# Four layers of windowed and full attention on one core: moving column maxima, first stores and the second keys

## The chip, the cores and the metric

The kernel runs on one core of a Trainium2 chip. A core has a matrix engine (PE), a vector engine (DVE), an engine for activation functions (ACT), a general engine (POOL) and an engine that here only starts transfers (SP). The engines run side by side, each through its own queue in order, and wait for each other by semaphores. Sixteen DMA engines move data between the core's memory and DRAM. Matrix products land in PSUM, a small memory of banks; a product may only start when the bank it writes has been read out.

The metric is the device time of one execution in microseconds. Before the change the median of three runs is 2730.53 us (2721.45 to 2735.32).

## The reference

The input is one sequence of 2048 rows of 512 numbers. Four layers are applied in turn: windowed (A), full (B), A, B, where the two A layers share their weights and so do the two B layers. A layer normalizes each row, projects to queries, keys and values (32 heads of 16), computes attention, projects with `wo` and adds the result to its input.

```python
def _B_ref(x, wqkv, wo):
    B, S, D = x.shape
    H = 32; Dh = D // H
    qkv = (lambda x, *d: x.transpose(*d))((x @ wqkv).reshape(B, S, 3, H, Dh), 2, 0, 3, 1, 4)
    q, k, v = qkv[0], qkv[1], qkv[2]
    scores = jnp.einsum("bhqd,bhkd->bhqk", q, k) * Dh ** -0.5
    p = _softmax(scores, axis=-1)
    o = jnp.einsum("bhqk,bhkd->bhqd", p, v)
    return (lambda x, *d: x.transpose(*d))(o, 0, 2, 1, 3).reshape(B, S, D) @ wo

x = A_x
x = x + _A_ref(_layernorm(x, axis=-1), A_wqkv, A_wo)
x = x + _B_ref(_layernorm(x, axis=-1), B_wqkv, B_wo)
x = x + _A_ref(_layernorm(x, axis=-1), A_wqkv, A_wo)
x = x + _B_ref(_layernorm(x, axis=-1), B_wqkv, B_wo)
```

`_A_ref` is the same with a mask: a query sees itself and the 255 rows before it.

## The kernel before

**Tiling.** The 2048 rows are cut into four columns (`c` = 0 to 3) of 512 queries. Heads are taken four at a time: `qd` = 0 to 7 counts these groups, and two of them in a row make a head pair's output `oh` (named `O[l, c, t]`, t = qd // 2). A layer's attention runs over c, then qd (in layer 3 over pairs of qd first). In a full layer one (c, qd) has 16 steps, one for each tile of 128 keys; in a windowed layer it has 3. A step computes scores on PE into a PSUM tile `s` (line 667), exponentials `e` on ACT (L671), in windowed layers masks on POOL (L734, L737), and two steps later the product with the values into the bank `acc` (L711 full, L744 windowed). At the end of a qd DVE transposes the sums (`ot`, L639), divides, and after every second qd writes `oh` (L652 to L655).

**Side work.** The projections of the next columns and layers are cut into pieces and laid between the steps by a planner (`Side`), which keeps a clock of estimated microseconds, gives each piece a cost, and takes the next one that is ready by its dependencies. Such a piece is a tile of 12 matmuls (L379 in windowed layers and in the prologue, L376 in full ones). `PH["run"]` says after how many matmuls of it a step of attention may follow: 12 in layer 0, 4 in layer 2. In full layers all side products go through one bank, `acc[1]`: the next tile's first matmul waits until DVE or ACT has copied the tile before out of it. Copies of values are L592 (ACT) and L594 (DVE, `vt`), of queries and keys L487 (ACT) or L489 (DVE) and L490 (DVE, `sp`).

Only PE's order is fixed by the planner. The order of the other engines, SP's transfers among them, is chosen by the framework's scheduler from the order of writing, priorities and its own estimates.

**Prologue.** Before the attention of layer 0, the kernel normalizes column 0, splits three weight matrices of type A into two half-precision parts (`parts`; matrix 1 holds the keys' weights, 0 the queries', 2 the values'), stores them to DRAM for later use (`wd`, L293, on SP's queue), computes keys, queries and values of column 0, and normalizes column 1. All loads and stores go through SP's queue, in order: where one waits, those behind it wait. The keys, queries and values of column 1 (`K(0,1)`, `Q(0,1)`, `VV(0,1)`, 48 matmuls each) are side work of column 0's attention. `kw` and `qs` are the DRAM homes of keys and queries, from which each qd loads `kt` and `qt` (L697 to L700 windowed, L684 to L688 full). `kt` has three buffers and `qt` two; x tiles have four.

**Column maxima.** The kernel checks that every column of the eight weight matrices has its largest magnitude in a range. `column_maxima` loads a matrix of 1 MB (`wq`, L277; the `wo` matrices in eight pieces, L282), after a tiny copy into the buffer (L275) that ties the load to another result; reduces it on DVE in four parts (`wa`, L311), transposes (L315) and reduces again (L317). All eight are work of the first half of layer 1's column 0, as two chains, and their loads are tied to the key maxima `KM[1]`, which are ready when layer 0's tail ends. In that half of layer 1 the upper value heads are side work too: 12 tiles, copied out by L594.

Of the kernel before, what the change touches and what calls it, by code (L numbers as in the profile page):

```python
# [11 lines left out]
F16 = mybir.dt.float16  # L12
# [7 lines left out]
P = 128  # L20
# [12 lines left out]
HEAD_START = 100  # L33
EB, XB, XNB, WB, VB, OB = 6, 4, 4, 2, 3, 5
RUN = 4
# [154 lines left out]
def fast_path(ctx, tc, flag, a_x, a_wqkv, a_wo, b_wqkv, b_wo, out):  # L190
# [29 lines left out]
    def wait(us):  # L220

        return "wait", clock[0] + us
# [62 lines left out]

    def parts(ty, s, raw):

        w = wp.tile([P, NC, 2, D], F16, name=f"w{ty}_{s}", tag="vf", bufs=NQ)
        for k in range(NC):
            nc.scalar.activation(w[:, k, 0, :], raw[:, k, :], AF.Copy, scale=UP[s])  # L290
            nc.vector.scalar_tensor_tensor(w[:, k, 1, :], raw[:, k, :], UP[s], w[:, k, 0, :], op0=ALU.mult, op1=ALU.subtract)
            yield
        nc.sync.dma_start(wd[ty, s], w)  # L293
        if ty == 0 and s < 3:
            WT[ty, s] = [w, w]
# [7 lines left out]
    def column_maxima(ty, s):  # L303

        yield wait(12)
        raw = load_w(ty, s, "vw", "wq", KM[1][:, NQ - 1:])
        yield wait(14)
        am = vp.tile([P, D], F32, name=f"wa{ty}_{s}", tag="am", bufs=1)
        for h in range(4):
            f = slice(h * P, (h + 1) * P)  # L310
            nc.vector.tensor_reduce(am[:, f], raw[:, :, f].rearrange("p k f -> p f k"), axis=AX.X, op=ALU.max,  # L311
                                    apply_absolute_value=True)
# [367 lines left out]
    def load_full(l, c, qd):  # L680
        n = f"{l}_{c}_{qd}"
        pair = slice(2 * qd, 2 * qd + 2)
        qt = pp.tile([P, 2, QC], F16, name=f"qt{n}", tag="qt", bufs=2)
        nc.sync.dma_start(qt, qs[1, c][pair].rearrange("r p n -> p r n"))  # L684
# [7 lines left out]
    def load_win(l, c, qd):  # L692
        n = f"{l}_{c}_{qd}"
        kt = pp.tile([P, 2, S // 2], F16, name=f"kt{n}", tag="kt", bufs=3)
        qt = pp.tile([P, 2, QC], F16, name=f"qt{n}", tag="qt", bufs=2)
        pair = slice(2 * qd, 2 * qd + 2)
# [205 lines left out]
    def run(g):  # L902
        for _ in g:
            pass
# [8 lines left out]
    def attention(l, works):  # L913
# [5 lines left out]
        for t in range(NHT if l == 3 else 1):  # L919
            for c in range(NQ):  # L920
# [9 lines left out]
                if win:  # L930
                    PH["run"] = RUN if l else 12
                ops = load(l, c, qds[0])
# [78 lines left out]
    def PR(ty, s, after=()):  # L1011
        return Work(prep(ty, s), 0.0, ("P", ty, s), after, aside=True)
# [18 lines left out]
    for i in range(4):  # L1031
# [6 lines left out]
        nc.vector.tensor_tensor(xl, pt, xh, ALU.subtract)  # L1038
    run(parts(0, 1, raw[1]))
    xs = load_x(0, 1)  # L1040
    run(keys(0, 0, True, None, True))
    run(parts(0, 0, raw[0]))
    for i in range(4):
# [4 lines left out]
    run(queries(0, 0, True))  # L1048
    run(parts(0, 2, raw[2]))
    vals = values(0, 0, True)  # L1050
# [3 lines left out]
    for d in [("P", 0, i) for i in range(3)] + [("K", 0, 0)]:  # L1054
        DONE[d] = 0.0

    def F(*parts):
# [7 lines left out]
    def side0(c):  # L1065
        if c == 0:
            return [F((kw[1], True), (qs[0, 1], False), (kw[2], True), (qs[0, 2], False)), K(0, 1), Q(0, 1), PR(0, 3, [("K", 0, 1)]), VV(0, 1), PR(1, 1, [("V", 0, 1, (0, 1), 0)]), NN(2, [("T", 0, 1)]), T(0, 2)]
        if c == 1:
# [38 lines left out]
    for i, m in enumerate(mats):  # L1107
        works[1][0].append(CM(*m, [("C", *list(mats)[i - 2])] if i > 1 else []))
    late = lambda l: [("N", l, 3)]
# [55 lines left out]
```

## Time and profile before

| What | Value |
|---|---|
| median of three runs | 2730.53 us (2721.45 to 2735.32) |
| profiled execution | 2732.19 us, of which the span from first to last instruction 2730.5 us |
| PE busy | 2607.2 us (95%), 24315 matmuls |
| ACT busy | 2371.7 us (87%) |
| DVE busy | 853.0 us (31%) |
| POOL busy | 521.9 us (19%) |
| mean granted PE clock | 0.989 |
| DMA | 353.14 MB, mean 129 GB/s |
| scores begin in layer 0, 1, 2 | 52.5 us, 477.8 us, 1449.8 us |

A row of the profile in order of time gives the start in microseconds from the span's start, the length of the merged group, engine and line, the operation, what it writes and reads, how many instructions were merged, and in brackets the idle time of the engine before it with what ended that time. The page's slices cut the span into 40 parts of 68 us; each digit is a busy share in tenths. Matmuls overlap, so a busy PE is not a PE at its peak. A row of the waits gives the waiting engine and line, what ended the wait, the total, the number of times and the longest.

### The profile page before, as it was taken

The page shows a single profiled execution, that of the slowest core. Times are in us where ns is not written, and L with a number is a line of the kernel's source. Part 1 is how long each engine was busy: PE and PEld are TensorE (multiplying, and loading weights), DVE is VectorE, ACT ScalarE, POOL GpSimd, SP SyncE. Part 2 cuts the span into 40 slices and gives each one's busy share as a digit, 9 for nine tenths or more (in the row PEclk, how much of TensorE's full clock was granted, in tenths as well). Part 3 has the DMA queues.
Part 4 walks back from the last instruction along what each step waited for, and adds up shares of the span by engine and source line. Part 5 has one row for each costly group of instructions (what it writes and reads, how often), then busy time and mean ns, then how long its engine had stood idle before and what let it go on. Part 6 is the DMA issues. An engine that isn't in the chain of part 4 may idle for free.

```text
span 2730.5 us, 59472 instructions
## 1 busy us (share of the span) xinstructions
PE 2607.2 (95%) x24315; PEld 758.9 (28%) x24315; DVE 853.0 (31%) x1941; ACT 2371.7 (87%) x2683; POOL 521.9 (19%) x1154
## 2 busy tenths in 40 slices
PE   7889999899999999999999999899999999999998
PEld 3233344222222222222223333422222222222221
DVE  6457454512121112111215576311222221121111
ACT  4566663799999999999997777499999999999997
POOL 1556551000000000000005688100000000000000
PEclk9999999899999999999999999999999999999999
DMA  8777866522232123212324666523333333333331
GB/s 271 226 233 242 243 201 213 159 78 85 86 101 88 58 90 109 79 69 82 109 73 136 195 171 177 159 76 101 110 113 127 126 108 111 95 110 115 99 95 56
DMA packets 322715, 353.14 MB, mean 129 GB/s; under 512 B 114432, under 2 KB 234496, under 8 KB 316416
## 3 DMA queue, kind: packets, MB, share of 16 engines
q1 hardware_dynamic: 322432, 349.25, 42.1%
q8 instruction: 192, 3.15, 0.5%
q14 instruction: 91, 0.75, 0.1%
HBM read 236.45 MB, written 96.99 MB: 122 GB/s over the span
## 4 chain that ended last, share of the span: by engine, by line
PE 74%; ACT 8%; DVE 7%; issue 5%; DMA 4%; SPq 1%; POOL 1%; ACTq 0%; DVEq 0%
PE acc L711 30%; PE s L667 20%; PE acc L376 10%; PE b L379 9%; ACT e L671 7%; PE acc L744 4%; PE bs L379 1%; DVE ot L639 1%; DVE wa L311 1%; DMA wv<-wd 1%; DVE xh L424 1%; DMA kt<-kw 1%; DVE xn L418 1%; DVE sp L490 1%; DMA qt<-qs 0%
## 5 line engine op out<-in xcount | busy, mean ns | idle before, releaser
L671 ACT ACTIVATE e<-s 128x1024 f32<-128x1024 f32 (+2 forms) x2432 | 2246.3, 1120 | 127.3 <-PE s L667 106.3
L711 PE MATMUL acc<-e,vt 128*17 128x512 f32 x8192 | 1082.4, 600 | 5.7 <-DVE ot L639 4.6
L667 PE MATMUL s<-qt,kt 64*128 64x512 f16 (+3 forms) x5504 | 774.6, 356 | 60.6 <-ACT e L671 23.9
L667 PEld LDWEIGHTS <-kt 64*128 64x128 f16 x5504 | 201.6, 94 | 807.3 <-issue 772.2
L737 POOL TENSOR_SCALAR_AFFINE_SELECT e<-e 128x256 f32<-128x256 f32 x512 | 229.5, 455 | 102.4 <-ACT e L671 101.7
L711 PEld LDWEIGHTS acc<-e,vt 128*17 128x17 f32 x8192 | 136.4, 95 | 384.3 <-issue 351.0
L639 DVE STREAM_TRANSPOSE ot<-acc 128x512 f32<-128x512 f32 x128 | 91.6, 715 | 455.2 <-PE acc L711 337.4
L734 POOL TENSOR_SCALAR_AFFINE_SELECT e<-e 128x256 f32<-128x256 f32 x448 | 201.7, 455 | 92.1 <-ACT e L671 88.5
L744 PE MATMUL acc<-e,vt 128*17 128x384 f32 (+2 forms) x2816 | 195.1, 390 | 0.0
L379 PE MATMUL b<-xc,w 128*128 128x512 f16 x700 | 166.2, 385 | 5.1 <-DVE km L528 4.9
L655 POOL TENSOR_TENSOR oh<-o,oh 128x512 f16<-128x512 f32 x31 | 36.0, 1161 | 706.6 <-DVE oh L654 643.3
L596 POOL TENSOR_SCALAR vt<-vt 128x16 f32<-128x16 f32 (+1 forms) x96 | 24.5, 256 | 475.9 <-DVE vt L594 306.5
L376 PE MATMUL acc<-xc,w_h 128*32 128x512 f16 x1296 | 108.5, 379 | 2.3 <-DVE km L528 2.3
L489 DVE TENSOR_SCALAR sp<-acc 128x512 f16<-128x512 f32 x28 | 19.3, 689 | 290.6 <-PE acc L376 278.9
L376 PE MATMUL acc<-xc,w 128*32 128x512 f16 x1344 | 108.9, 379 | 0.0
L487 ACT ACTIVATE sp<-b 128x512 f16<-128x512 f32 x59 | 35.3, 598 | 84.3 <-PE b L379 74.5
L489 DVE TENSOR_SCALAR sp_h<-acc 128x512 f16<-128x512 f32 x27 | 18.6, 690 | 283.5 <-PE acc L376 283.5
L627 DVE SCALAR_TENSOR_TENSOR x<-acc,x 128x512 f32<-128x512 f32 x60 | 41.5, 692 | 206.1 <-PE acc L376 198.2
L379 PEld LDWEIGHTS <-w 128*128 128x128 f16 x800 | 73.6, 99 | 114.5 <-issue 37.3
L376 PE MATMUL acc<-wv,xc 128*32 128x256 f16 (+1 forms) x1728 | 94.8, 313 | 9.8 <-DVE vt L594 9.8
L495 POOL TENSOR_TENSOR sq_h<-sp_h 128x512 bf16<-128x512 f16 x27 | 28.1, 1041 | 389.9 <-DVE sp_h L489 389.9
L376 PE MATMUL acc<-wo,oh 128*32 128x512 f16 x1296 | 101.3, 379 | 0.0
(133 smaller groups left out, 1518.9 us busy)
## 6 DMA issues: line engine op xcount, KB each, us to landing
kt<-kf SPq DMA_DIRECT2D x128, 512.0 KB
qt<-qs SPq DMA_DIRECT2D x128, 256.0 KB
xd<-x SPq DMA_DIRECT2D x96, 256.0 KB
x<-xd SPq DMA_DIRECT2D x96, 256.0 KB
w<-wd SPq DMA_DIRECT2D x20, 1024.0 KB
kt<-kw SPq DMA_DIRECT2D x64, 256.0 KB
qs<-sp SPq DMA_DIRECT2D x48, 256.0 KB
wo<-wd SPq DMA_DIRECT2D x12, 1024.0 KB
```

The source lines that it names most:

```text
L376: nc.tensor.matmul(ps[g:g + 32], a[:, g:g + 32], b, start=(i == 0), stop=(i == len(pairs) - 1), skip_group_check=True)
L379: nc.tensor.matmul(ps, a, b, start=(go and i == 0), stop=(i == len(pairs) - 1))
L489: nc.vector.tensor_scalar(sp[:, 0], ps, e, None, op0=ALU.mult)
L627: nc.vector.scalar_tensor_tensor(xs[i], ps, 1.0 / (UP[2] * UP[3]), xs[i], op0=ALU.mult, op1=ALU.add)
L639: nc.vector.transpose(ot.rearrange("p b r -> p (b r)"), a)
L655: (nc.gpsimd if l % 2 and (l, c, qd) != (3, NQ - 1, NQD - 1) else nc.vector).tensor_tensor(hl[:, 1], o, hl[:, 0], ALU.subtract)
L667: nc.tensor.matmul(ps[:, h, s0:s0 + wd_], kt[R * h:R * h + R, pr, kc:kc + P], qt[R * h:R * h + R, pr, qc:qc + wd_], start=True, stop=True)
L671: nc.scalar.activation(e[:, :, w0:w1], ps[:, :, w0:w1], AF.Exp, scale=SCALE)
L711: nc.tensor.matmul(a[32 * h:32 * h + DH + 1, :], V[l, qd // 4, j // 8][:, j % 8, 4 * (qd % 4) + h, :], es_[h // 2][:, h % 2, :], start=(j ...
L734: nc.gpsimd.affine_select(v, v, pattern=[[0, 2], [-1, P]], compare_op=ALU.is_gt, fill=0.0, base=0, channel_multiplier=1)
L737: nc.gpsimd.affine_select(v, v, pattern=[[0, 2], [1, P]], compare_op=ALU.is_ge, fill=0.0, base=0, channel_multiplier=-1)
L744: nc.tensor.matmul(a[32 * h:32 * h + DH + 1, q * P:(q + nb) * P], V[l, (4 * c + j) // 4][:, j % 4, 4 * qd + h, :], es_[h // 2][:, h % 2, s ...
```

## The change

Five edits:

- `K(0,1)` is run to its end in the prologue, before layer 0's attention, and is no longer side work of column 0.
- The three first stores of split weights are issued on POOL's queue.
- In column 0 of layer 0 side tiles are cut after 4 matmuls, as in layer 2.
- Column maxima i = 0 to 7 are tied to the head pair output `O[1, 0, i // 2]` of layer 1, by planner and by the tiny copy before the load; each odd one also waits for the even one before it. The first two stay in the first half of column 0, the others follow in the rest of the layer.
- `qt` gets three buffers, x tiles five.

```diff
-EB, XB, XNB, WB, VB, OB = 6, 4, 4, 2, 3, 5
+EB, XB, XNB, WB, VB, OB = 6, 5, 4, 2, 3, 5
...
-    def parts(ty, s, raw):
+    def parts(ty, s, raw, eng=None):
...
-        nc.sync.dma_start(wd[ty, s], w)
+        (eng or nc.sync).dma_start(wd[ty, s], w)
...
     def column_maxima(ty, s):
 
-        yield wait(12)
-        raw = load_w(ty, s, "vw", "wq", KM[1][:, NQ - 1:])
+        i = list(mats).index((ty, s))
+        raw = load_w(ty, s, "vw", "wq", O[1, 0, i // 2][:, 0, :1])
...
-        qt = pp.tile([P, 2, QC], F16, name=f"qt{n}", tag="qt", bufs=2)
+        qt = pp.tile([P, 2, QC], F16, name=f"qt{n}", tag="qt", bufs=3)
...
-                    PH["run"] = RUN if l else 12
+                    PH["run"] = RUN if l or not c else 12
...
-    run(parts(0, 1, raw[1]))
+    run(parts(0, 1, raw[1], nc.gpsimd))
...
-    run(parts(0, 0, raw[0]))
+    run(parts(0, 0, raw[0], nc.gpsimd))
...
-    run(parts(0, 2, raw[2]))
+    run(parts(0, 2, raw[2], nc.gpsimd))
...
         DONE[d] = 0.0
+    all_of([K(0, 1)])
...
-            return [F((kw[1], True), (qs[0, 1], False), (kw[2], True), (qs[0, 2], False)), K(0, 1), Q(0, 1), PR(0, 3, [("K", 0, 1)]), VV(0, 1), PR(1, 1, [("V", 0, 1, (0, 1), 0)]), NN(2, [("T", 0, 1)]), T(0, 2)]
+            return [F((kw[1], True), (qs[0, 1], False), (kw[2], True), (qs[0, 2], False)), Q(0, 1), PR(0, 3, [("K", 0, 1)]), VV(0, 1), PR(1, 1, [("V", 0, 1, (0, 1), 0)]), NN(2, [("T", 0, 1)]), T(0, 2)]
...
     for i, m in enumerate(mats):
-        works[1][0].append(CM(*m, [("C", *list(mats)[i - 2])] if i > 1 else []))
+        works[1][0 if i < 2 else 1].append(CM(*m, [("O", 1, 0, i // 2)] + [("C", *list(mats)[j]) for j in (i - 1,) if i % 2]))
```

The edits also move instructions in the queues. The first place is ACT's queue where layer 0's attention begins (`vt` is the last value copy of column 0, `sp_1_1` and `sq_1_1` the copies and squares of the keys of column 1, `e` the exponentials of qd 0). Before:

```order
L592 ACTIVATE vt_0_0_0_461<-b_520 128x32x16
L671 ACTIVATE e_0_0_0_0_546<-s_0_0_0_0_543 128x2x384
L671 ACTIVATE e_0_0_0_1_553<-s_0_0_0_1_550 128x2x384
L487 ACTIVATE sp_1_1_0_580<-b_567 128x512
L671 ACTIVATE e_0_0_1_0_590<-s_0_0_1_0_587 128x2x256
L493 ACTIVATE sq_1_1_0_583<-sp_1_1_0_580 128x512
L671 ACTIVATE e_0_0_1_1_596<-s_0_0_1_1_593 128x2x256
L487 ACTIVATE sp_1_1_1_612<-b_599 128x512
```

After:

```order
L592 ACTIVATE vt_0_0_0_461<-b_520 128x32x16
L487 ACTIVATE sp_1_1_0_548<-bs_535 128x512
L493 ACTIVATE sq_1_1_0_551<-sp_1_1_0_548 128x512
L487 ACTIVATE sp_1_1_1_568<-b_555 128x512
L493 ACTIVATE sq_1_1_1_571<-sp_1_1_1_568 128x512
L487 ACTIVATE sp_1_1_2_588<-bs_575 128x512
L493 ACTIVATE sq_1_1_2_591<-sp_1_1_2_588 128x512
L487 ACTIVATE sp_1_1_3_608<-b_595 128x512
L671 ACTIVATE e_0_0_0_0_626<-s_0_0_0_0_623 128x2x384
L493 ACTIVATE sq_1_1_3_611<-sp_1_1_3_608 128x512
L671 ACTIVATE e_0_0_0_1_633<-s_0_0_0_1_630 128x2x384
```

The copies of the keys stood between the exponentials of qd 0 to 2 and now stand ahead of them, as their matmuls do on PE.

The second place is SP's queue after the fills of the key and query homes, before:

```order
L269 DMA qs_0_97<-ones 32x15x512
L293 DMA wd_1_106<-w_1_206 128x4096
L437 DMA x_4_216<-in_A_x_dram 128x512
L437 DMA x_5_218<-in_A_x_dram 128x512
L437 DMA x_6_220<-in_A_x_dram 128x512
```

and POOL's queue between its constants and the first masks, after:

```order
L253 AFFINE_SELECT hsum<-hsum 128x32
L293 DMA wd_1_106<-w_1_206 128x4096
L293 DMA wd_0_105<-w_0_304 128x4096
L293 DMA wd_2_107<-w_2_451 128x4096
L596 TENSOR_SCALAR vt_0_0_0_461<-vt_0_0_0_461 128x32 x4
L737 AFFINE_SELECT e_0_0_0_0_626<-e_0_0_0_0_626 128x2x128
```

The stores left SP, where x tiles of column 1 stood behind the first of them, for the head of POOL's queue; there the ones beside the values (L596) and the first masks stand behind all three.

The third place is DVE's queue in the first column of layer 1. Before, in qd 0 to 1 (`wq` a loaded matrix, `vt_1_0` copies of values from `acc[1]`):

```order
L594 COPY vt_1_0_5814<-acc_82 128x16x16
L315 STREAM_TRANSPOSE wb_0_7324<-wa_0_7287 128x512
L275 COPY wq_3_7333<-km_3958 128x1
L311 TENSOR_REDUCE wa_1_7289<-wq_1_7175 128x128 x4
L317 TENSOR_REDUCE cmax<-wb_0_7324 128x16
L315 STREAM_TRANSPOSE wb_1_7326<-wa_1_7289 128x512
L317 TENSOR_REDUCE cmax<-wb_1_7326 128x16
L311 TENSOR_REDUCE wa_2_7343<-wq_2_7330 128x128 x4
```

After, behind the output of the first head pair (`oh_0_1`):

```order
L654 CAST oh_0_1_6605<-o_0_1_6603 128x512
L275 CAST wq_0_6678<-oh_0_1_6605 128x1
L275 CAST wq_1_7148<-oh_0_1_6605 128x1
L594 COPY vt_1_0_5814<-acc_82 128x16x16
L311 TENSOR_REDUCE wa_0_6889<-wq_0_6678 128x128 x4
L315 STREAM_TRANSPOSE wb_0_7110<-wa_0_6889 128x512
L317 TENSOR_REDUCE cmax<-wb_0_7110 128x16
L311 TENSOR_REDUCE wa_1_7257<-wq_1_7148 128x128
L594 COPY vt_1_1_5651<-acc_82 128x16x16
L311 TENSOR_REDUCE wa_1_7257<-wq_1_7148 128x128 x3
```

and behind that of the third (`oh_0_5`; `sp_0_3_0` is a query copy of column 3):

```order
L275 CAST wq_0_8101<-oh_0_5_8036 128x1
L275 CAST wq_1_8465<-oh_0_5_8036 128x1
L311 TENSOR_REDUCE wa_0_8265<-wq_0_8101 128x128 x4
L315 STREAM_TRANSPOSE wb_0_8423<-wa_0_8265 128x512
L317 TENSOR_REDUCE cmax<-wb_0_8423 128x16
L311 TENSOR_REDUCE wa_1_8629<-wq_1_8465 128x128 x4
L315 STREAM_TRANSPOSE wb_1_8794<-wa_1_8629 128x512
L317 TENSOR_REDUCE cmax<-wb_1_8794 128x16
L489 TENSOR_SCALAR sp_0_3_0_8188<-acc_82 128x512
```

The eight maxima stood as one run among the value copies of qd 0 and 1. Now two stand behind each head pair's output, the first two still ahead of a value copy, the fifth and sixth ahead of a query copy.

SP's queue moves with them: the first two of these loads (`wq`) stand among the query and key loads of qd 3 and 4 of layer 1, and in the full layers the `qt` load of a qd stands between the key loads of the qd before it. In layer 0's column 0 the eight loads of `wo` stand between the key stores of column 1, and the x loads of column 2 behind them. In column 1 a load of a type B matrix (`wr`) that stood ahead of the values' weights `wv` of column 2 stands behind them.

More of the change, by code (lines that the diff above doesn't have):

```diff
@@ L694, in load_win @@
         kt = pp.tile([P, 2, S // 2], F16, name=f"kt{n}", tag="kt", bufs=3)
-        qt = pp.tile([P, 2, QC], F16, name=f"qt{n}", tag="qt", bufs=2)
+        qt = pp.tile([P, 2, QC], F16, name=f"qt{n}", tag="qt", bufs=3)
         pair = slice(2 * qd, 2 * qd + 2)
```

## The prediction

> **What bounds the kernel now.** I read the page's table of slices first, then the stretches of layer 1, the matmuls and loads of layer 0 in order of time, and the waits. The program has four layers: windowed attention (0, 2) and full attention (1, 3). In the slices ACT is at nine tenths through both full layers and at four to seven in the windowed ones, where the DMA engines are busiest:
>
> ```profile
> ACT  4566663799999999999997777499999999999997
> DMA  8777866522232123212324666523333333333331
> ```
>
> So layers 1 and 3 run at the rate of the exponentials (L671), and little of the change touches that, except at the start of layer 1. Counted in stretches of 40 us (exponentials in brackets, then clock, DMA share, GB/s), that start is slower than what follows:
>
> ```profile
> 480.00:520.00 40.00, 35.11 (x39) 0.91 0.61 173
> 520.00:560.00 40.00, 30.44 (x33) 0.87 0.43 105
> ...
> 600.00:640.00 40.00, 40.00 (x45) 1.00 0.14 46
> ```
>
> 39 and 33 exponentials stand against 45, with a lower clock: here the eight column maxima run. The other place is the beginning of layer 0. PE's matmuls in order of time (start, length, group, the idle time before it and who ended it):
>
> ```profile
> 46.09 2.75 PE L379 MATMUL b<-w,xc 128*128 128x512 f16 x12
> 52.52 0.50 PE L667 MATMUL s<-qt,kt 64*128 64x384 f16 x4 [3.67 <-DMA qt<-qs]
> ...
> 94.50 0.50 PE L667 MATMUL s<-qt,kt 64*128 64x384 f16 x4 [3.06 <-DMA kt<-kw]
> ...
> 95.89 4.00 PE L379 MATMUL b<-xc,w 128*128 128x512 f16 x12
> ...
> 131.27 0.61 PE L667 MATMUL s<-qt,kt 64*128 64x128 f16 x8 [2.70 <-DMA qt<-qs]
> ...
> 132.37 4.45 PE L379 MATMUL b<-xc,w 128*128 128x512 f16 x12
> ...
> 189.16 5.14 PE L379 MATMUL b<-wv,xc 128*128 128x512 f16 x12 [5.48 <-DMA wv<-wd]
> ```
>
> PE waits for loads, and the twelve matmuls behind such a wait take 4.00, 4.45 and 5.14 us instead of 2.75: 1.25, 1.7 and 2.4 us of slow clock on top of 3.06, 2.70 and 5.48.
>
> **Part 1: the second keys before the attention, side work in fours in its first column.** Before, keys, queries and values of column 1 (3 x 48 matmuls) stand inside column 0's attention, twelve at a time. After, the 48 of the keys stand ahead of it and 96 remain, four at a time. The trace of before holds that second arrangement: layer 2's column 0 has the same 24 steps and 96 side matmuls in fours. Its first scores, those of its column 1, and a later wait in that layer:
>
> ```profile
> 1449.78 0.50 PE L667 MATMUL s<-qt,kt 64*128 64x384 f16 x4
> ...
> 1506.09 0.61 PE L667 MATMUL s<-qt,kt 64*128 64x128 f16 x8 [1.78 <-DMA kt<-kw]
> ...
> 1589.86 0.89 PE L667 MATMUL s<-qt,kt 64*128 64x128 f16 x8 [2.57 <-DMA kt<-kw]
> ```
>
> That is 56.3 us. Before, PE is through with its prologue at 46.09 + 2.69 = 48.8, idles 3.67, and column 1 begins at 131.27. After, the keys fill 48.8 to 59.6 (48 x 2.70/12 = 10.8), which covers the wait for qt, and 56.3 later it is 115.9: 15.4 us earlier. Column 0's queries end near its middle, so column 1's qt is no longer the late one, and 1.7 us of slow clock go: 17.1. What is late next are column 0's own loads: in SP's queue each pair of them (qt, kt) now stands behind a query tile's two stores, which come from PE's fourth step before; and third weights, x tiles and stores come in less time. Bounds: 18.9 (no 1.78 either) and 4 (three pairs late at 3.06 + 1.25 each). I take **14**, three less than the analogue, since the loads of layer 0 compete with more.
>
> What moves with it: ACT's four key copies and squares now precede the exponentials; they hide beside the keys' matmuls. The preparation of the wo weights starts at once, its eight loads lie between the key stores; the x loads of tiles 8 to 11 come behind them, some 10 us later, and their transposes are due a column later, so nothing waits for that.
>
> **Part 2: the three first stores on POOL's queue.** The stores on SP before, two late loads, and what SP waited for with the first:
>
> ```profile
> 17.80 0.34 SPq L293 DMA_DIRECT2D wd<-w  x1
> ...
> 45.16 0.44 SPq L293 DMA_DIRECT2D wd<-w  x1
> ...
> 177.69 0.45 SPq L277 DMA_DIRECT2D wr<-in_B_wqkv_dram  x1
> 178.24 0.50 SPq L340 DMA_DIRECT2D wv<-wd  x1
> ```
> ```profile
> SPq L293 <- DVE w L291: 7.6, 1, 7.6
> ```
>
> SP is freed of a 7.6 us wait and the x tiles of column 1 come that much earlier; but PE works without a gap there, so I count **0**. POOL issues three; no row shows POOL issuing one. The nearest is SP's 0.34 to 0.44 us each; the far end is that POOL is held until the third store's time, 45.16. Its first mask comes after 59.6, so even that costs nothing. [...]
>
> The order of SP changes further on: the values' weights (wv, issued at 178.24) stood behind a 1 MB load (177.69); now that load comes after them. Of 5.48 + 2.4 us I take **3**; ends 0 and 7.9, nearer to 0, because two stores of 1 MB stay ahead.
>
> **Part 3: the column maxima.** PE in the same stretch, DVE there (maxima wa, value copies vt, later output halves oh and query copies sp), PE after one query tile, SP's first load, and two pieces of the chain:
>
> ```profile
> 477.80 1.46 PE L667 MATMUL s<-qt,kt 64*128 64x512 f16 x6 [4.79 <-DMA kt<-kf]
> ...
> 496.96 0.73 PE L376 MATMUL acc<-wv,xc 128*32 128x256 f16 x20 [2.51 <-DVE vt L594]
> ...
> 523.84 0.73 PE L376 MATMUL acc<-wv,xc 128*32 128x256 f16 x20 [2.24 <-DVE vt L594]
> ...
> 525.04 1.90 PE L711 MATMUL acc<-e,vt 128*17 128x512 f32 x8
> ...
> 530.33 1.05 PE L711 MATMUL acc<-e,vt 128*17 128x512 f32 x8
> ...
> 536.16 1.26 PE L376 MATMUL acc<-wv,xc 128*32 128x256 f16 x20 [3.15 <-DVE vt L594]
> ...
> 563.17 0.73 PE L376 MATMUL acc<-wv,xc 128*32 128x256 f16 x20 [1.88 <-DVE vt L594]
> ```
> ```profile
> 474.02 3.79 DVE L311 TENSOR_REDUCE wa<-wq 128x128 f32<-128x512 f32 x4 [7.52 <-DMA wq<-in_A_wqkv_dram]
> ...
> 485.75 4.01 DVE L311 TENSOR_REDUCE wa<-wq 128x128 f32<-128x512 f32 x4 [6.47 <-DMA wq<-in_A_wqkv_dram]
> ...
> 491.14 3.96 DVE L311 TENSOR_REDUCE wa<-wq 128x128 f32<-128x512 f32 x4
> ...
> 585.82 0.42 DVE L594 COPY vt<-acc 128x256 f32<-128x256 f32 x1 [8.72 <-PE acc L376]
> ...
> 593.21 0.42 DVE L594 COPY vt<-acc 128x256 f32<-128x256 f32 x1 [3.98 <-PE acc L376]
> ...
> 619.36 0.43 DVE L654 CAST oh<-o 128x512 f16<-128x512 f32 x1
> 628.14 0.69 DVE L489 TENSOR_SCALAR sp<-acc 128x512 f16<-128x512 f32 x1 [8.36 <-PE acc L376]
> ...
> 679.22 0.43 DVE L654 CAST oh<-o 128x512 f16<-128x512 f32 x1
> 689.85 0.69 DVE L489 TENSOR_SCALAR sp<-acc 128x512 f16<-128x512 f32 x1 [10.20 <-PE acc L376]
> ```
> ```profile
> 631.05 0.83 PE L376 MATMUL acc<-xc,w 128*32 128x512 f16 x12
> ```
> ```profile
> 466.48 0.74 SPq L277 DMA_DIRECT2D wq<-in_A_wqkv_dram  x1
> ```
> ```profile
> 434.30 5.35 DMA w<-wd
> 467.31 6.26 DMA kf<-mk_None
> ```
>
> One maximum holds DVE for 491.14 - 485.75 = 5.4 us; a value copy queued behind it comes late, its PSUM bank stays taken, and PE with all behind it stands: 2.51 + 2.24 + 3.15 + 1.88 = 9.8 us, and slow matmuls (1.90 for 1.05) after three of them, about 1.8 each: 15 us in all. That goes.
>
> It comes back smaller. Each load now waits for a head pair's output, and DVE's reduces wait for the load, ahead of copies in DVE's order. A load of 1 MB takes 5.35 us (434.30). Pair 1: the first load lands 5.4 behind the casts, its maximum ends at 10.8, one reduce of the second follows, and the value copy behind it, due after 593.21 - 585.82 = 7.4, comes at 11.9: 4.5 late. PE comes to the bank 631.05 - 628.14 = 2.9 us after a copy begins, and a query tile's two copies take 1.4, so 1.5 are slack: 3.0 of stall and 1.8 of slow clock. Pair 2: 5.4 + 5.4 after 619.8 is 630.6 for a copy due at 628.14: 1.0 beyond the slack, which ACT covers from the two score tiles PE is ahead (1.8). Pair 3: both maxima stand before the copy due at 689.85; 679.7 + 5.4 + 10.8 = 695.9 is 6.0 late: 4.5 of stall, 1.8 covered, 1.8 of slow clock. Pair 4 has three reduces before such a copy: nothing. That is 9.3; I take 11, because a load can take the 7.5 us from 466.48 to 474.02, which adds 2 to each pair (the far end is 17). Net **4** less.
>
> [...]
>
> The first 1 MB load (466.48) also stood ahead of the key shift's stores, which took 6.26 us and which the first kt load needs; PE then idled 4.79. Without it I take **3**, ends 0 and 4.8.
>
> **Part 4: three query buffers, five x buffers.** In the full layers kt's three buffers stop SP at the same point: 0. In layer 2 the kt loads get past qt's wait; of 1.78 + 2.57 I take **2** (0 to 4.4). The fifth x buffer moves a load by one place: 0.
>
> **Sum:** 14 + 0 + 3 + 4 + 3 + 2 = 26. The profiled execution took 2732.2 us, 1.7 above the median 2730.5; against that median I forecast 2705.
>
> **Rivals.** *The maxima cost what they did* (loads of 7.5 us: 17 us come back, and 15 go): 2711. For it: DVE now waits for each load at four places. Against it: at most one block lies in a dense stretch.
> *The loads of column 0 come late* (three pairs): part 1 gives 4 and the sum 16, so 2715; with part 2's 3 us gone too, 2718. For it: the DMA share of 7 to 8 tenths; against it: in layer 2's analogue a single pair was late.
> *Slower:* the DMA engines are the bound of layer 0, and the compressed queue makes loads late one after the other in columns 0 and 1 (16 pairs), at 4.3 us each. From the sixth late pair (26/4.3) nothing is left; with ten it is 2748. Against it: before, three loads were late at nearly the same share.
> *POOL's stores are held up:* column 2's key weights read what POOL stored, and the keys then wait as the values did (5.48 + 2.4): 2713. [...]
>
> **How the numbers follow.** Forecast 0.50, maxima 0.18, late loads 0.18, slower 0.08, POOL 0.06. The range reaches from 2690 (the large ends of parts 1 to 3) to 2730 (all three gains at their small ends). Half a per cent, what a measurement of this kernel can tell, is 13.7 us: below 2716.9 lie the forecast, most of the maxima's case, a third of the late loads: 0.68; slower by that much only a part of the fourth case: 0.06; the rest 0.26.
>
> **What would show it.** Column 1's first scores near 116 instead of 131.27; no idle time of PE above 2 us between 50 and 116; wv's wait at half; the first scores of layer 1 about 3 us nearer to the last matmul of layer 0; 44 to 45 exponentials in each 40 us of layer 1 but one or two, where PE waits for DVE behind a maximum. I am wrong if loads end PE's waits in column 0, or if those waits behind maxima sum to over 15 us.

## The result and the profile after

The changed kernel takes 2734.03 us (median of 12 runs, 2730.00 to 2738.42), the kernel before 2731.34 us in the same comparison (12 runs, 2721.45 to 2737.10). The ratio is 1.0009, 95% interval 0.9997 to 1.0020: no difference that can be measured, where 2705 was forecast. The profiled execution took 2736.46 us with a span of 2734.7, so it lies 2.4 us above its median. One run among the experiments below, of `after_sp`, took 3210.65 us at a granted clock of 0.751 and is not in that kernel's ratio.

The slices of ACT and of the DMA engines after the change:

```profile
ACT  4565664999899999999997777499999999999997
DMA  7789866224332223212323656623334333333331
```

ACT's third to sixth slice are no denser than before, and behind the first slices of layer 1 there is now an 8 (slice 11, 684 to 752 us) where nines stood. Exponentials per 40 us, then clock, DMA share and GB/s, in the changed kernel:

```profile
480.00:520.00 40.00, 36.02 (x39) 0.91 0.29 87
520.00:560.00 40.00, 39.93 (x44) 1.00 0.39 133
560.00:600.00 40.00, 34.22 (x38) 0.91 0.20 67
...
680.00:720.00 40.00, 33.42 (x37) 0.91 0.24 83
720.00:760.00 40.00, 33.31 (x38) 0.91 0.50 139
```

The stretch at 520 has 44 exponentials where it had 33. Three later stretches have 37 or 38 and a clock of 0.91: what the maxima cost at the start of the layer they now cost behind it.

PE in the prologue, in the two columns of layer 0 that the change was to shorten, and in layer 1:

```profile
33.30 0.58 PE L512 MATMUL b<-sq,hsum 128*32 128x512 bf16 x1 [4.10 <-ACT sq L493]
33.82 5.26 PE L379 MATMUL bs<-xc,w 128*128 128x512 f16 x12
...
65.35 0.50 PE L667 MATMUL s<-qt,kt 64*128 64x384 f16 x4
...
104.17 0.82 PE L667 MATMUL s<-qt,kt 64*128 64x384 f16 x4 [7.39 <-DMA kt<-kw]
...
129.11 0.82 PE L667 MATMUL s<-qt,kt 64*128 64x384 f16 x4 [3.53 <-DMA kt<-kw]
...
138.36 0.40 PE L667 MATMUL s<-qt,kt 64*128 64x128 f16 x4 [0.29 <-ACT e L671]
...
194.05 5.30 PE L379 MATMUL b<-wv,xc 128*128 128x512 f16 x12 [4.50 <-DMA wv<-wd]
...
482.88 1.46 PE L667 MATMUL s<-qt,kt 64*128 64x512 f16 x6 [3.10 <-DMA kt<-kf]
...
562.39 1.05 PE L376 MATMUL acc<-wv,xc 128*32 128x256 f16 x16 [3.50 <-DVE vt L594]
...
626.97 0.83 PE L376 MATMUL acc<-xc,w 128*32 128x512 f16 x12 [1.71 <-DVE sp L490]
...
693.17 1.47 PE L376 MATMUL acc<-xc,w 128*32 128x512 f16 x12 [4.44 <-DVE sp L490]
...
753.71 1.47 PE L376 MATMUL acc<-wo,oh 128*32 128x512 f16 x12 [4.60 <-DVE m_None L540]
```

Column 1's first scores come at 138.36, not near 116. Two waits for `kt` (7.39, 3.53) stand in column 0 where one of 3.06 stood, and the prologue has a wait that it did not have (4.10, with twelve matmuls in 5.26 us behind it).

The places in the program at which the kernels can be compared are the first scores and the head pairs' outputs (DVE's cast `oh`, L654). Times in us from the span's start, in the profiled executions; the last four columns are kernels of the next section:

| place | before | after | after_m_before | after_norm | norm_no_cm | norm_m_sums |
|---|---|---|---|---|---|---|
| first scores, layer 0 | 52.5 | 65.4 | 58.6 | 60.2 | 59.2 | 63.2 |
| first scores of column 1 | 131.3 | 138.4 | 132.5 | 122.5 | 121.1 | 123.0 |
| last output of layer 0 | 421.3 | 428.2 | 419.7 | 409.8 | 407.4 | 412.9 |
| first scores, layer 1 | 477.8 | 482.9 | 476.2 | 463.8 | 462.5 | 468.4 |
| layer 1, column 0, pair 1 | 559.5 | 548.8 | 556.1 | 530.6 | 527.9 | 534.7 |
| pair 2 | 619.4 | 613.4 | 617.3 | 594.4 | 586.3 | 593.1 |
| pair 3 | 679.2 | 675.2 | 677.2 | 655.9 | 646.2 | 652.9 |
| pair 4 | 738.9 | 741.3 | 736.6 | 721.4 | 705.6 | 712.4 |
| column 1, pair 1 | 797.7 | 807.4 | 795.4 | 784.4 | 764.4 | 771.1 |
| last output of layer 2 | 1715.7 | 1724.5 | 1710.6 | 1701.8 | 1682.5 | 1687.1 |
| last output | 2717.4 | 2722.8 | 2711.5 | 2702.4 | 2680.9 | 2688.6 |

Read as differences: layer 0 ends 6.9 us later. From there to pair 1's output 17.6 us are gained (120.6 instead of 138.2). From pair 1 to column 1's pair 1, 20.3 are lost (258.5 instead of 238.2). Up to layer 2's last output 0.9 more are gained, and 3.0 between it and layer 3's first pair (not in the table); at the last output the changed kernel is 5.4 us later.

### The profile page after: what moved, and what is told of

Same layout as the page of the kernel before. It is cut to its first block, busy times and chain, and to the rows that moved or that the text cites. A ratio compares the mean times of both kernels' runs of the same rounds, so it can differ in the third digit from the quotient of the medians.

```text
span 2734.7 us, 59474 instructions
## 1 busy us (share of the span) xinstructions
PE 2608.4 (95%) x24315; PEld 755.3 (28%) x24315; DVE 855.3 (31%) x1941; ACT 2373.1 (87%) x2683; POOL 523.1 (19%) x1157
## 4 chain that ended last, share of the span: by engine, by line
PE 75%; ACT 8%; DVE 6%; DMA 5%; issue 4%; SPq 1%; POOL 1%; ACTq 0%; DVEq 0%
PE acc L711 30%; PE s L667 19%; PE acc L376 10%; PE b L379 9%; ACT e L671 7%; PE acc L744 4%; PE bs L379 2%; DVE ot L639 1%; DMA wv<-wd 1%; DMA kw<-sp 1%; DMA wq<-in_A_wqkv_dram 1%; DVE wa L311 1%; DMA kt<-kw 1%; DMA wq<-in_B_wqkv_dram 0%; SPq L445 0%
## 5 line engine op out<-in xcount | busy, mean ns | idle before, releaser
L671 ACT ACTIVATE e<-s 128x1024 f32<-128x1024 f32 (+2 forms) x2432 | 2246.6, 1111 | 150.6 <-PE s L667 131.7
L379 PE MATMUL b<-xc,w 128*128 128x512 f16 x676 | 159.5, 381 | 3.7 <-DVE km L528 3.7
L596 POOL TENSOR_SCALAR vt<-vt 128x16 f32<-128x16 f32 (+1 forms) x96 | 24.4, 255 | 437.8 <-DVE vt L594 294.5
L495 POOL TENSOR_TENSOR sq<-sp 128x512 bf16<-128x512 f16 x28 | 29.1, 1041 | 380.0 <-DVE sp L489 380.0
L594 DVE COPY vt<-acc 128x256 f32<-128x256 f32 (+1 forms) x36 | 18.5, 514 | 254.5 <-PE acc L376 254.5
```

What stands on the lines that cost most here:

```text
L379: nc.tensor.matmul(ps, a, b, start=(go and i == 0), stop=(i == len(pairs) - 1))
L495: nc.gpsimd.tensor_tensor(sq, sp[:, 0], sp[:, 0], ALU.mult)
L671: nc.scalar.activation(e[:, :, w0:w1], ps[:, :, w0:w1], AF.Exp, scale=SCALE)
```

## The experiments

**The waits in column 0: a query copy behind the normalization.** In the changed kernel's trace, SP issues nothing between 82.81 and 99.41 us, and DVE is busy without a gap from 80.87 on. SP's queue, its longest wait, and the ends of DVE's run (L291 weights, L398 to L424 the normalization of column 2, L490 a query copy):

```profile
82.81 0.42 SPq L267 DMA_DIRECT2D kw<-zeros  x1
99.41 0.34 SPq L503 DMA_DIRECT2D qs<-sp  x1
99.80 0.43 SPq L504 DMA_DIRECT2D qs<-sp  x1
100.33 0.39 SPq L697 DMA_DIRECT2D qt<-qs  x1
100.76 0.49 SPq L698 DMA_DIRECT2D kt<-kw  x1
```
```profile
SPq L503 <- DVE oh L654: 16.4, 1, 16.4
```
```profile
80.87 0.69 DVE L291 SCALAR_TENSOR_TENSOR w<-wr,w 128x512 f16<-128x512 f32 x1 [0.49 <-ACT w L290]
81.48 1.28 DVE L398 BATCH_NORM_STATS2 st<-x 128x6 f32<-128x512 f32 x2
...
97.30 0.89 DVE L424 TENSOR_TENSOR xh<-xn,xh 128x512 f16<-128x512 f32 x1
98.11 0.70 DVE L652 STREAM_TRANSPOSE o<-op 128x512 f32<-128x512 f32 x1
98.74 0.65 DVE L490 SCALAR_TENSOR_TENSOR sp<-b,sp 128x512 f16<-128x512 f32 x1
```

The query copy ends at 98.74 + 0.65 = 99.39, and the store that needs it goes out at 99.41; the profile names `oh`, which began in the same half microsecond. Behind the store stands the `kt` load for which PE waits 7.39 us. So the theory is a chain through three queues: normalization ahead of a query copy on DVE, its store at the head of SP, the loads behind it. The rival is that the DMA engines are too busy for these loads. The experiment adds one dependency to the normalization (the loads of its x tiles move with it, from 69.60 to 95.19 us):

```diff
-NN(2, [("T", 0, 1)])
+NN(2, [("T", 0, 1), ("Q", 0, 1)])
```

> The changed kernel with the normalization of column 2 made to follow the queries of column 1 and not only their input, so that in DVE's queue it stands behind the last query copy. Theory (the 7.39 us wait for kt comes from a query copy queued behind the normalization on DVE, whose store holds SP): that wait goes with its slow matmuls, column 1's scores begin 8 to 12 us earlier than 138.4, and the time is 2722 to 2729. Rival (the DMA engines are late whatever the order): a wait for kt or qt over 4 us stays in the second half of column 0, and the time is over 2731.

Measured: 2720.84 us, ratio 0.9960 (0.9949 to 0.9970), a little below the range of the theory. The waits that are left in column 0:

```profile
99.88 0.50 PE L667 MATMUL s<-qt,kt 64*128 64x384 f16 x4 [0.36 <-DMA kt<-kw]
...
106.90 0.50 PE L667 MATMUL s<-qt,kt 64*128 64x384 f16 x4 [0.43 <-DMA kt<-kw]
...
122.45 0.61 PE L667 MATMUL s<-qt,kt 64*128 64x128 f16 x8 [2.48 <-DMA kt<-kw]
```

No wait for a load over 0.5 us is left in column 0, and column 1 begins 62.3 us after the first scores (122.45 - 60.20) instead of 73.0. The same `kt` loads through the same engines are in time when the copy is. The changed kernel's own trace speaks against the rival too: between 87 and 99 us, while SP waited, the DMA share is 0.00. The queue was the cause, not the DMA engines' load.

**The first stores.** The prologue's wait of 4.10 us follows a key copy on ACT that waits until an earlier key copy is stored (both use the three `sp` buffers). POOL had issued three stores of 1 MB by then:

```profile
17.63 0.75 POOL L293 DMA_DIRECT2D wd<-w  x1 [14.69 <-DVE w L291]
20.04 0.54 POOL L293 DMA_DIRECT2D wd<-w  x1 [1.66 <-DVE w L291]
23.60 0.53 POOL L293 DMA_DIRECT2D wd<-w  x1 [3.02 <-ACT sp L487]
```
```profile
31.99 0.60 ACT L487 ACTIVATE sp<-b 128x512 f16<-128x512 f32 x1 [6.14 <-DMA kw<-sp]
```

One run puts the stores back on SP, the other puts them on POOL's queue in the kernel before:

```diff
-    run(parts(0, 1, raw[1], nc.gpsimd))
+    run(parts(0, 1, raw[1]))
...
-    run(parts(0, 0, raw[0], nc.gpsimd))
+    run(parts(0, 0, raw[0]))
...
-    run(parts(0, 2, raw[2], nc.gpsimd))
+    run(parts(0, 2, raw[2]))
```

> The changed kernel with the three first stores back on SP's queue, the rest unchanged. Theory (three stores of 1 MB started by 23.6 us hold up the key stores, whose buffer the fourth key copy needs): ACT's wait of 6.14 us and PE's of 4.10 go, with 2.5 us of slow matmuls; the first scores come at 58.5 to 60 instead of 65.35; the time is 2726 to 2731. Rival (the early x loads or the order of the key stores are the cause): the wait stays over 3 us and the first scores come after 63.

Measured: 2734.56 us, ratio 1.0010 (0.9997 to 1.0023). The first scores came at 58.77 as the theory had it, and ACT's wait was 1.10 instead of 6.14; but the time, given as 2726 to 2731, did not move. The changed kernel with the old maxima suggests why: it has its stores on POOL, yet its first scores came at 58.64. So the wait of 4.10 belongs, it seems, to the execution that was profiled. Over all profiles, ACT's longest such wait was 1.4 to 6.1 us in eight of nine kernels with the stores on POOL and none in the ninth, of which PE lost 0 to 4.1, and 0 to 1.2 us in the five with the stores on SP.

```diff
-    run(parts(0, 1, raw[1]))
+    run(parts(0, 1, raw[1], nc.gpsimd))
```

(the same for matrices 0 and 2)

> The kernel before with the three first stores on POOL's queue alone. The prediction counted 0, and as a rival a POOL that is held up. Theory: POOL issues the stores at once, the key stores behind them take longer, PE idles 0 to 4 us in the prologue, partly taken up by the wait for qt that follows; 2730 to 2737. Rival (POOL is held up by DVE or by issuing, and layer 0's masks are late): first scores after 60, over 2737.

Measured: 2723.45 us, ratio 0.9980 (0.9968 to 0.9992): a small gain, where theory and rival had none. In the profiled execution PE did lose 3.4 us in the prologue and the first scores came at 52.72, since the wait of 3.67 for `qt` fell away in exchange. The gain lies behind it: column 1's first scores came at 126.78 instead of 131.27, with waits for loads of 1.32 and 2.18 us where 3.06 and 2.70 stood. Why this does not show between the changed kernel and the one with its stores on SP was not settled; there the query copy sets when the loads go out, in both.

**The maxima: what the change alone gives, and what it had taken.**

> The kernel before with the column maxima's edit alone. Theory (the maxima's cost came back at four places of layer 1): the first head pair's output of layer 1 is some 15 to 18 us earlier than before, the first of its column 1 some 3 us later, and PE waits behind DVE at three or four places for 3.5 to 4.6 us each; the time is 2728 to 2736. Rival (the 20 us that came back belong to the other edits, the loads moved by the third query buffer above all): pairs 1 to 4 give back 11 at most, the time is 2721 to 2727.

In the kernel before:

```diff
-        yield wait(12)
-        raw = load_w(ty, s, "vw", "wq", KM[1][:, NQ - 1:])
+        i = list(mats).index((ty, s))
+        raw = load_w(ty, s, "vw", "wq", O[1, 0, i // 2][:, 0, :1])
...
-        works[1][0].append(CM(*m, [("C", *list(mats)[i - 2])] if i > 1 else []))
+        works[1][0 if i < 2 else 1].append(CM(*m, [("O", 1, 0, i // 2)] + [("C", *list(mats)[j]) for j in (i - 1,) if i % 2]))
```

It took 2732.76 us, ratio 1.0010 (0.9995 to 1.0026). Against the end of its layer 0, pair 1 came 17.6 us earlier, and pairs 2 to 4 and column 1's first pair gave back 3.8 + 4.7 + 5.8 + 4.2 = 18.5. PE's waits from 470 to 820 us in that kernel:

```profile
PE acc L376 <- DVE sp L490: 7.0, 2, 4.1
PE acc L376 <- DVE vt L594: 3.6, 1, 3.6
...
PE acc L376 <- DVE m_None L540: 2.4, 1, 2.4
```

These are 13.0 us of idle time. The rest goes with a slower clock: the mean granted clock from pair 1 to column 1's first pair is 0.97 there and 1.00 in the kernel before. So the return belongs to the maxima's edit alone, not to the loads that the query buffers move. The other way round, with these lines reversed in the changed kernel:

> The changed kernel with the column maxima as they were. Theory (the edits are independent): layer 0 ends 6.9 us later than before as it does in the changed kernel, layer 1 loses nothing more and gains nothing, layer 3 begins 3 us nearer; the time is 2731 to 2736. Rival (layer 0's loss comes from the maxima's loads or order): layer 0 ends earlier than 426 and the time is below 2728.

Measured: 2728.11 us, ratio 0.9989 (0.9977 to 1.0000). The time is below the range given and at the rival's bound, and layer 0 ends before 426 as the rival had it: at 419.7, 8.6 us earlier than in the changed kernel and 1.6 earlier than before. But 6.7 of these 8.6 us are already there at the first scores (58.64 for 65.35), and PE's wait in the prologue varies among the kernels with the old maxima too (0, 2.2 and 3.4 us in the three that have the stores on POOL); so most of the 6.9 us is put down to that one execution. What the maxima's edit does to the rest of layer 0, some 2 us here, was not settled. The waits for `kt` in column 0 are there all the same (11.6 us in three).

Three kernels with the normalization moved, `after_norm` being one of them, then give the maxima's price. The first of the other two leaves out the column maxima altogether, loads, reduces and the check of the range:

```diff
-        works[1][0 if i < 2 else 1].append(CM(*m, [("O", 1, 0, i // 2)] + [("C", *list(mats)[j]) for j in (i - 1,) if i % 2]))
+        pass
...
-            return [Work(column_range(), 0.0, None, [("C", *m) for m in mats], aside=True), OO(1, 3), Q(2, 2), T(2, 3)]
+            return [OO(1, 3), Q(2, 2), T(2, 3)]
...
-    nc.vector.tensor_mul(okay[:, 0:1], okay[:, 0:1], okay[:, 2:3])
```

> The changed kernel with the normalization of column 2 behind the queries of column 1, and with the column maxima left out altogether (their loads, reduces and the check of their range). Theory (the maxima's price is PE waiting for DVE at four places, 18 to 20 us together): some 18 us below the same kernel with maxima (2720.8), 2700 to 2706, with a full rate of exponentials through layer 1's first column. Rival (what was lost there is the load on SP and the DMA engines, or belongs to other work): less than 8 us, over 2712.

The second has the maxima as they were before, by the lines above reversed:

> As the changed kernel with the normalization behind the queries, but the column maxima as they were before. Theory (both places of the maxima cost the same, 17.6 against 18.5 to 20.3 us): 2715 to 2721, and layer 0 ends 10 to 13 us earlier than before. Rival (the norm's gain hangs on the maxima's new place): over 2725.

Measured: 2698.78 us without maxima, a little below the range, ratio 0.9873 (0.9857 to 0.9890), and 2718.43 us with the maxima as before, ratio 0.9934 (0.9914 to 0.9954). From the ratios, the maxima cost (0.9934 - 0.9873) x 2730 = 17 us at their old place and (0.9960 - 0.9873) x 2730 = 24 at their new one, give or take 7 and 5 by the intervals. The new place is no better than the old one, and perhaps worse.

**What makes the price.** In the changed kernel's DVE queue, the first reduce behind each pair's output waits for its load:

```profile
554.70 4.02 DVE L311 TENSOR_REDUCE wa<-wq 128x128 f32<-128x512 f32 x4 [4.26 <-DMA wq<-in_A_wqkv_dram]
...
620.14 3.99 DVE L311 TENSOR_REDUCE wa<-wq 128x128 f32<-128x512 f32 x4 [6.08 <-DMA wq<-in_A_wqkv_dram]
...
681.00 4.03 DVE L311 TENSOR_REDUCE wa<-wq 128x128 f32<-128x512 f32 x4 [5.17 <-DMA wq<-in_B_wqkv_dram]
...
750.19 2.87 DVE L311 TENSOR_REDUCE wa<-wq 128x128 f32<-128x512 f32 x3 [8.20 <-DMA wq<-in_B_wqkv_dram]
```

If only the place in the queue costs, a maximum should be free where nothing urgent stands behind it. The first try reduces in two halves, each tied to a copy out of the bank that is written after the load (`COPY` holds the newest such copy):

```diff
         am = vp.tile([P, D], F32, name=f"wa{ty}_{s}", tag="am", bufs=1)
-        for h in range(4):
-            f = slice(h * P, (h + 1) * P)
+        for h in range(2):
+            f = slice(2 * h * P, 2 * (h + 1) * P)
+            seen, tries = COPY[0], 0
+            while COPY[0] == seen and tries < 100:
+                tries += 1
+                yield wait(0.4)
+            nc.vector.tensor_copy(am[:, 2 * h * P:2 * h * P + 1], COPY[1])
             nc.vector.tensor_reduce(am[:, f], raw[:, :, f].rearrange("p k f -> p f k"), axis=AX.X, op=ALU.max,
                                     apply_absolute_value=True)
-            yield wait(2)
```

> As the changed kernel with the normalization behind the queries, and each maximum reduced in two halves, each tied to a copy out of the product bank that was written after the load (a tiny copy from that copy's tile into the result), so that DVE doesn't wait for a load and each block (2 us, then 3.4 us) lies right behind a copy. Theory (only the place in DVE's queue costs): PE's waits behind DVE in the first column of layer 1 go but for less than 4 us in all, the time is 2702 to 2709. Rival (the 1 MB loads or DVE's busy time as such cost): 2714 or more.

Measured: 2707.52 us, ratio 0.9902 (0.9886 to 0.9919). The time is in the theory's range, and so are PE's waits for DVE in the first column, 3.3 us in all. But those for value and query copies are gone and waits for the sums' transposition (`ot`) have come, in the second column too: 7.0 us up to 900 us, the longest 3.4. Two maxima stood in a row behind one copy there. The next kernel lets each copy carry one half:

```diff
-            while COPY[0] == seen and tries < 100:
+            while COPY[0] in (seen, COPY[2]) and tries < 100:
...
+            COPY[2] = COPY[0]
```

> As the kernel with halves of maxima behind copies, but each copy now carries one half at most, so that no two maxima stand in a row ahead of the sums' transposition (ot). Theory (3.3 and 4.0 us were lost in layer 1 where a second maximum followed behind the same copy): those two waits of PE for ot go and the time is 2698 to 2704. Rival (the remainder is the loads' or the reduces' own price): no change, 2705 to 2710.

Measured: 2708.39 us, ratio 0.9929 (0.9913 to 0.9946): no gain, and the waits for `ot` are 8.3 us. My reading was wrong: not the second maximum but the place is the trouble. DVE and PE in that kernel (here L497 and L498 are the query copy, L320 a half, L649 `ot`):

```profile
673.01 0.69 DVE L497 TENSOR_SCALAR sp<-acc 128x512 f16<-128x512 f32 x1 [11.01 <-DMA kt<-kf]
673.73 0.69 DVE L498 SCALAR_TENSOR_TENSOR sp<-acc,sp 128x512 f16<-128x512 f32 x1
...
674.65 1.91 DVE L320 TENSOR_REDUCE wa<-wq 128x256 f32<-128x1024 f32 x1
676.48 0.70 DVE L649 STREAM_TRANSPOSE ot<-acc 128x512 f32<-128x512 f32 x1
```
```profile
677.23 1.05 PE L721 MATMUL acc<-e,vt 128*17 128x512 f32 x8 [2.27 <-DVE ot L649]
```

Query copies come some 15 us apart and sums some 30, and each second copy lies just ahead of the sums. A half of 1.91 us put there makes `ot` late by about as much, and PE waits 2.27. The same kernel with its first stores on SP, by the same lines as in `after_sp`:

> The same with the three first stores back on SP's queue. Theory (the stores on POOL's queue make a key copy wait for the key stores by 1.4 to 6.1 us, of which PE loses 0 to 4; all else equal): 0 to 3 us below the same kernel with stores on POOL. Rival (SP freed of its 7.6 us wait is worth something): 2 us above or more.

Measured: 2705.88 us, ratio 0.9912 (0.9892 to 0.9932); the intervals overlap, so the stores' queue makes no difference that shows.

The last kernel ties a whole maximum to a head group's sums (`op`, or `oh` where a pair is complete), one to each group, and all eight to the second half of column 0 and later:

```diff
+        seen, tries = SUM[0], 0
+        while SUM[0] in (seen, SUM[2]) and tries < 160:
+            tries += 1
+            yield wait(0.4)
+        SUM[2] = SUM[0]
         for h in range(4):
             f = slice(h * P, (h + 1) * P)
+            nc.vector.tensor_copy(am[:, h * P:h * P + 1], SUM[1])
             nc.vector.tensor_reduce(am[:, f], raw[:, :, f].rearrange("p k f -> p f k"), axis=AX.X, op=ALU.max,
                                     apply_absolute_value=True)
-            yield wait(2)
...
             ONR[l, c, t] = clock[0] + 4.5
+        SUM[:2] = SUM[0] + 1, hl[:, 0, :1] if u else OT[t][:, 0, 0, :1]
...
-        works[1][0 if i < 2 else 1].append(CM(*m, [("O", 1, 0, i // 2)] + [("C", *list(mats)[j]) for j in (i - 1,) if i % 2]))
+        works[1][1].append(CM(*m, [("O", 1, 0, i // 2)] + [("C", *list(mats)[j]) for j in (i - 1,) if i % 2]))
```

> As the changed kernel with the normalization behind the queries, and each maximum whole (four reduces, transposition, last reduce: 5.4 us) tied to the sums of a head group that come after its load, one maximum for each group of heads, all eight from the fifth group of column 0 on. In the kernels with halves behind copies every second copy stands 1.9 us ahead of the sums' transposition (ot), and PE waited 1.4 to 2.3 us for ot there, 7 to 8 us in all; behind the sums the next copy is some 13 us away. Theory (only what stands next in DVE's queue costs): PE's waits for DVE in the first two columns of layer 1 fall from 8 us to under 3, layer 1's second column begins within 3 us of the kernel without maxima; the time is 2697 to 2703 on a chip where the kernel before takes 2730. Rival (a block of 5.4 us is too long anywhere, or the loads have a price of their own): over 2706.

Measured: 2698.91 us (5 runs, 2697.10 to 2701.91), ratio 0.9889 (0.9872 to 0.9906). DVE around one maximum (L644 `ot`, L317 three of its four reduces, L322 its last reduce, L494 the next query copy), and all of PE's waits for DVE from 470 to 900 us:

```profile
620.15 0.72 DVE L644 STREAM_TRANSPOSE ot<-acc 128x512 f32<-128x512 f32 x1 [2.04 <-PE acc L717]
...
622.24 3.03 DVE L317 TENSOR_REDUCE wa<-wq 128x128 f32<-128x512 f32 x3
...
627.22 0.69 DVE L322 TENSOR_REDUCE cmax<-wb 128x16 f32<-128x512 f32 x1
631.68 0.69 DVE L494 TENSOR_SCALAR sp<-acc 128x512 f16<-128x512 f32 x1 [3.78 <-PE acc L381]
```
```profile
PE acc L717 <- DVE ot L644: 0.9, 3, 0.3
```

The same loads and the same reduces, with PE waiting 0.9 us for DVE, as in the kernel without maxima. In the table this kernel loses nothing between pair 1 and column 1's pair 1 (236.5 us; 236.5 without maxima; 238.2 before). By the ratios it is 4 us above the kernel without maxima, give or take 7. So neither the 1 MB loads nor DVE's time has a price that shows here; what costs is what stands next in DVE's queue. This version is 1.1% (0.9 to 1.3) faster than the kernel before, and faster than the change.

**The buffers.** Three `qt` and five `x` buffers alone, in the kernel before:

```diff
-EB, XB, XNB, WB, VB, OB = 6, 4, 4, 2, 3, 5
+EB, XB, XNB, WB, VB, OB = 6, 5, 4, 2, 3, 5
...
-        qt = pp.tile([P, 2, QC], F16, name=f"qt{n}", tag="qt", bufs=2)
+        qt = pp.tile([P, 2, QC], F16, name=f"qt{n}", tag="qt", bufs=3)
```

(the second in both load functions)

> The kernel before with three query buffers and five x buffers alone. The prediction had 2 us less, from the waits for kt in layer 2. Theory (those waits aren't shortened; in the changed kernel layer 2 took 0.4 us less up to its last column): 2729 to 2733. Rival (the 3 us that layer 3's beginning came nearer in the changed kernel belong to the buffers): 2726 to 2729, and layer 3's first head pair 3 us nearer to layer 2's end.

Measured: 2730.41 us, ratio 0.9988 (0.9974 to 1.0002), so between 7 us less and nothing, which holds the 2 us of the prediction and doesn't show them. Layer 3's first pair came 0.6 us nearer to layer 2's end, not 3. The 3 us in the changed kernel's trace lie elsewhere (last section).

## Why the prediction was wrong

**Part 1, 14 us less: wrong, and here the forecast fell.** In the changed kernel with the old maxima, whose prologue ran undisturbed, the scores began at 58.64 (forecast 59.6) and column 1's at 132.46 (forecast 116 to 117). Column 0 took 73.8 us and not the 56.3 of layer 2. The step that failed is the sentence that the x loads of tiles 8 to 11 come later and "nothing waits for that". They came 17 us later (69.60 instead of 52.00), and nothing waited for their result; but the normalization that they feed moved with them, from ahead of the queries on DVE (it ran from 60 to 76 us before) to the middle of them (81 to 98 us), and a query copy, its store and the next loads stood behind it. I had named the pairs of loads behind a query tile's stores on SP as what would be late next, and priced them at 3.06 + 1.25 us each from PE's side; I didn't follow the stores back to the copies that they wait for and to what stands ahead of those in DVE's order. The analogue of layer 2 has no normalization of this kind in its column 0. With that one dependency added, column 0 takes 62.3 us, and column 1 begins 8.8 us earlier than before. The 6 us that are still missing against layer 2's 56.3 are for the larger part waits of the scores for exponentials (L671), 4.7 us against 1.3 in layer 2's column 0: a term that the prediction didn't have, and whose cause was not looked into.

The rival *late loads of column 0* came nearest in kind: loads were late, two of them, but for this reason and not for the DMA share that I had put behind it; its 2715 to 2718 is 16 us or more below what was measured. Of my two signs of being wrong the first came true, loads ended PE's waits in column 0; PE's waits behind maxima sum to 14.2 us, under the 15 of the second. Against the rival *slower* speaks `after_norm`, where the same loads in the compressed queue are in time. Of *POOL's stores are held up* nothing was seen; POOL issued them in 0.53 to 0.75 us each, within a microsecond of their weights being split. (The chance of 0.68 for a time below 2716.9 left this rival out, whose 2713 lies below it too.)

**Part 2, 0 and 3 us less: small either way.** For POOL's issue the row gives 0.53 to 0.75 us where I took 0.34 to 0.44 from SP's. What the three stores do to the key stores was not in the sum at all: I counted their issue and not their 3 MB beside the key stores. It costs PE 0 to 4 us in the prologue by execution. The wait for `wv` fell from 5.48 to 4.50 in the profile after and to 2.17 with the old maxima, so 0.8 to 5.7 us with the clock of the matmuls behind it, against 3 taken. The kernel before with this part alone was 2 to 9 us faster, which I had not forecast.

**Part 3, what goes: right.** From layer 1's first scores to pair 1's output, 65.96 us after and 81.69 before: 15.7 less, 15 forecast. The first scores of layer 1 came 1.9 us nearer to layer 0's last output, and 2.8 in the kernel with this part alone; 3 forecast.

**Part 3, what comes back: mis-sized, 11 against 20.3** (18.5 with this part alone). By pairs, in the order of the forecast 4.8, 0, 4.5 and 0: 4.7, 1.9, 6.5 and 7.3. Pair 1 came out as worked. Pair 4 failed: I let it go because three reduces stand before such a copy, and the profile after has the load landing 8.20 us late for DVE, then these three, and PE's wait of 4.60 behind the shift copy `m` (L540). I had also let ACT cover 1.8 us in pairs 2 and 3; the 40 us behind pair 3 have 37 exponentials where 45 fit, so little seems to have been covered. The rival *maxima cost what they did* (17 us come back) was the better forecast of this part.

**Part 4, 2 us less:** between 7 less and nothing, so neither borne out nor refuted.

Put together: of the 26 us, 14 of part 1 didn't come, 9 of part 3 came back on top, and the rest is within what executions differ by.

## What to carry to other kernels

When a change moves a load, follow what it feeds down to the engine's queue: work that nobody waits for still delays whatever urgent work ends up behind it there, and through a store at the head of a transfer queue that can be the loads of another engine (here SP issued nothing for 16.4 us, and PE waited 7.39 for `kt`). Off-path work (here eight maxima of 5.4 us each, on an engine that is 31% busy) costs by the instruction that stands next in the queue: ahead of a copy that PE was waiting for, the eight cost some 20 us in all; behind the sums, with the next copy almost 10 us after the start of the one shown, nothing that these runs can tell. To place such work, tie it by data to the instruction that opens the longest gap, and let it start after its load has landed.

## What the runs showed of the hardware

**The same pause costs nothing or some 1.5 us.** In layer 0's column 1, PE pauses for the key maximum at the same point of every kernel, for 2.4 to 2.6 us. The twelve matmuls behind it take 2.75 us in eight of the fourteen profiles and 4.00 to 4.44 in six. In the 4 us behind the pause the granted clock is 1.00 in each of the eight and 0.57 to 0.67 in the six. Two of them, of the changed kernel and of the one with the old maxima:

```profile
167.25 2.75 PE L379 MATMUL b<-xc,w 128*128 128x512 f16 x12 [2.51 <-DVE km L528]
```
```profile
161.33 4.44 PE L379 MATMUL b<-xc,w 128*128 128x512 f16 x12 [2.50 <-DVE km L528]
```

The 3 us that the changed kernel gained behind layer 2's last output are for the larger part of this kind: there twelve matmuls took 4.44 us behind a wait of 3.17 for `wo` before, and 2.75 behind one of 2.30 after. Behind the key maximum the pauses are 2.39 to 2.56 us in the six slowed profiles and 2.38 to 2.56 in the eight others, so their length doesn't decide it; what does, no run here shows.

**Key stores released their buffers later with the first stores on POOL's queue.** The three stores of 1 MB on POOL's queue took 8.4 us from issue to landing (median), so in the changed kernel they were under way from 17.63 to about 32 us, with a DMA share of 0.92 in that stretch. The key stores that SP issued meanwhile (from 21.76 us on) released their buffers late, by 6.14 us in the worst of nine profiles and not at all in one, against 1.2 us at most in the five with those stores on SP. Before, the second and third of the three stood behind the key stores on SP and were issued at 32.01 and 45.16 us, and the DMA share from 17.80 to 32.00 was 0.74. How the DMA engines divide their time between the two queues, no run here shows.
